# Nine selections per group moved from GpSimd to VectorE, the counting of the blocks put first, and three fp32r warm-up products

## The chip, the cores and the metric

One core of a Trainium2 chip. The metric is the device time of one execution in microseconds (us); lower is better. The engines are named as in the profile: PE is TensorE (PEld its weight loads), DVE is VectorE, ACT is ScalarE, POOL is GpSimd, SP is SyncE, which here only starts transfers.

## The reference

A linear attention with exponential features over 8 batches, 8 heads and 576 positions feeds a mixture of 8 experts that takes, for each of its 4608 tokens, the one expert with the largest logit.

```python
def phi(x):
    proj = np.einsum('bhsd,df->bhsf', x, w_phi)
    proj = proj - np.max(np.abs(proj), axis=-1, keepdims=True)
    return np.concatenate([np.exp(proj), np.exp(-proj)], axis=-1)
q_p, k_p = (phi(q), phi(k))
kv = np.einsum('bhsf,bhsd->bhfd', k_p, v)
z = np.sum(k_p, axis=2)
num = np.einsum('bhsf,bhfd->bhsd', q_p, kv)
den = np.einsum('bhsf,bhf->bhs', q_p, z)[..., None] + 1e-06
...
logits = x @ w_gate                       # x: num / den, 4608 x 512
expert_idx = np.argmax(logits, axis=1)
...
    h = np.maximum(xe @ w1[e], 0.0)       # xe: the tokens of expert e
    ye = h @ w2[e]
    out[mask] = gate_w[mask, None] * ye
```

## The kernel before

**Attention.** The heads are worked in 16 units `u` of two heads for two batches, four units to a group, so that a group holds the nine 128-token tiles of two batches with all heads. Every float32 matrix is split into a rounded part and a remainder (names that end in `h` and `l`, or `_hi` and `_lo`), and a product is three products: high by high, high by low, low by high. In a unit `project` (L253 to L260) multiplies a tile of k or q by the weights into the PSUM tile `ps_proj` (two buffers); DVE takes the largest magnitude `mx` (L259) and subtracts it (`t`, L260); ACT takes the exponentials. For k, ACT rounds them to `kh` (L280) and DVE or POOL subtracts to `kl` (L282); for q, PE transposes `t` into `pt` (L291) first. PE sums k by v in `pk` (L334), the sums are multiplied with a constant in `pf` (L360), DVE copies them to `kf` (L370), and `pn` (L382) multiplies the q features with `kf`. `normalize` (L409 to L418) divides on DVE. POOL splits the inputs (`xl`, L242).

**Routing.** When a group's four units are done, `route` turns its logits into a choice of expert and a rank of each token within its expert. For the first three groups (`final` is None) its steps are spread between the products of the next group's first unit, so one falls near 145, 245 and 345 us. The last of these steps are nine calls of `select(c)` (L734), one per tile: each makes two bfloat16 matrices of 128x128 from the row `iota_pb` and the tile's ranks `rkr`, `sel_p` on DVE and `sel_h` on POOL. The last group is routed by two more calls, `r1` and `r2`, in the transition to the experts (about 415 to 450 us); there some selections are made on ACT, and the four others stay as they are.

**Transition.** From the counts of all tokens, `place` (L552 to L589) works out which blocks of 128 rows belong to which expert; `block_of` (L909 to L928) gives each token its block as the matrix `bsel`; `tokens_of` (L935 to L944) sums 72 small products of `sel_p` and `sel_h` with `bsel` into `pp`, from which DVE reads the token lists `gidx` and `sidx`; `experts_of` (L946 to L964) finds the expert of each block: four compares into `eg` (L955, DVE), two steps on POOL (L961, L962), and the sum `eidx` (L964, DVE). The SP queue reads `eidx` before it starts the conditional weight transfers of the pair of blocks 2 (L981, L984).

**Experts.** Blocks are worked in pairs. `gather` fetches the rows of a block by `gidx` with a transfer that POOL issues (L845); `x_parts` transposes them (`px`, L1021) and splits them to `xh` (L1023, ACT) and `xl` (L1024, DVE); `pair_first` multiplies by the first matrix (`pm`, L1041 to L1043) and splits the result to `hh`, `hl` (L1049); `pair_second` multiplies by the second (`po`, L1061 to L1063); `write` scales and scatters. `weights(u, k)` splits piece k (0 to 7) of an expert's matrices: `wh` on ACT (L998), `wl` (L999) on POOL for the pieces in a list, else on DVE. The first two pairs use an expert that was chosen early, whose weights and rows are there before the transition.

**Start.** Seven bfloat16 products of 512 columns (L118) into a scratch PSUM tile come ahead of the first projection.

**What sets the order.** The program is written in the order in which the steps are called; a scheduler then moves instructions within each engine by priorities and its own model of their lengths. `tc.high_priority` raises the priority of what is called in it; the kernel ties some orders by dependencies without a semaphore (`add_manual_dep`). Each engine then runs its list strictly in order.

Of the kernel before, what the change touches and what calls it, by code (L numbers as in the profile page):

```python
# [42 lines left out]
XW = DM + 4  # L43

WARM = 7
BIG = 8192.0


@with_exitstack
def tile_linear_attention_moe(  # L50
# [65 lines left out]
    for _ in range(WARM):  # L116
        pw = ps_kv.tile([P, 4, P], F32, name="pw", tag="pk")
        T.matmul(pw, ones, ones.unsqueeze(1).to_broadcast([P, 4, P]), start=True, stop=True)  # L118
    iota_i = const.tile([P, P], I32, name="iota_i")
    iota_p = const.tile([P, P], F32, name="iota_p")  # L120
    iota_pb = const.tile([P, P], BF16, name="iota_pb")
# [313 lines left out]

    behind_order = [None]

    def ordered(items):


        def go(f):
            m = f()
            if behind_order[0] is not None:
                tc.add_manual_dep(
                    m.ins,
                    behind_order[0].ins.name,
                    mybir.DependencyInfo(mybir.DependencyClass.NoSync, mybir.DependencyReason.DATA),
                    reason="order of the products",
                )
            behind_order[0] = m  # L450

        return [(t, lambda f=f: go(f)) for t, f in items]
# [141 lines left out]
    def route(g, lgc, c0, n, final=None):  # L594
# [77 lines left out]
        def count():  # L672
            if final:
                pc = ps_kv.tile([P, E], F32, name="pc", tag="pk")
                T.matmul(pc, ones, r["base_b"], start=True, stop=False)
                for c in range(n):
                    T.matmul(pc, ones, r["oh_b"][:, c, :], start=False, stop=(c == n - 1))
                place(pc)

        def sum_up():  # L680
            if not final:
# [48 lines left out]
        def select(c):  # L730
            if final is not None and c0 + c in ON_ACT:
                return select_a(c)
            for eng, dst, by in ((V, sel_p, part1), (G, sel_h, hbase[:, j0 + c : j0 + c + 1])):
                eng.tensor_scalar(  # L734
                    dst[:, j0 + c, :], iota_pb, r["rkr"][:, c : c + 1], by, op0=ALU.is_equal, op1=ALU.mult
                )
# [198 lines left out]
    def tokens_of():  # L935

        pp = ps_kv.tile([P, NB], F32, name="pp", tag="pk")
        for j in range(NTILE):
            T.matmul(pp, sel_p[:, j, :], bsel[:, j, :], start=(j == 0), stop=False)
            T.matmul(pp, sel_h[:, j, :], bsel[:, j, :], start=False, stop=(j == NTILE - 1))  # L940
        V.tensor_scalar(gidx, pp, -1.0, 0.0, op0=ALU.add, op1=ALU.max)
        emp = sg.tile([P, NB], F32, name="emp")
        V.tensor_scalar(emp, pp, 0.5, BIG, op0=ALU.is_lt, op1=ALU.mult)
        V.scalar_tensor_tensor(sidx, pp, -1.0, emp, op0=ALU.add, op1=ALU.add)  # L944

    def experts_of():  # L946
        ends = sg.tile([1, 2, E], F32, name="ends")
# [4 lines left out]
        places = ((first[0:1], ends[:, 0], 0, 2 * NPAIR), (start[0:1], ends[:, 1], 2 * NPAIR, NB))  # L952
        for low, high, n0, n1 in places:
            for j, edge in enumerate((low, high)):
                V.tensor_tensor(  # L955
                    eg[:, j, n0:n1],
                    iota_p[0:1, n0:n1].unsqueeze(2).to_broadcast([1, n1 - n0, E]),
                    edge.unsqueeze(1).to_broadcast([1, n1 - n0, E]),
                    op=ALU.is_ge,
                )  # L960
        G.tensor_tensor(eg[:, 0], eg[:, 0], eg[:, 1], op=ALU.subtract)  # L961
        G.tensor_tensor(eg[:, 0], eg[:, 0], iota_e[0:1].unsqueeze(1).to_broadcast([1, NB, E]), op=ALU.mult)  # L962
        with nc.allow_low_precision("experts are integers"):
# [3 lines left out]
    st = {}  # L967
    lim = [NU_ALWAYS]

    POOL_LO0, POOL_LO = (1, 3, 7), (3, 7)  # L970

    def blocks(u):
        return [2 * u, 2 * u + 1] if u < NPAIR else [u + NPAIR]
# [13 lines left out]
    def weights(u, k):  # L987
# [8 lines left out]
        th = pool.tile([P, FF], F32R, name="wh", tag=f"wh{slot}")  # L996
        tl = pool.tile([P, FF], F32R, name="wl", tag=f"wl{slot}")
        A.copy(th, raw[k])  # L998
        (G if k in (POOL_LO if u else POOL_LO0) else V).tensor_tensor(tl, raw[k], th, op=ALU.subtract)  # L999
        for j in range(2) if u == 0 else [u]:  # L1000
            st["w", j, k] = (th, tl)
        if u > 0:
# [46 lines left out]
        V.scalar_tensor_tensor(hl, pm, 0.0, hh, op0=ALU.max, op1=ALU.subtract)  # L1049
        st["hp", u, j] = (hh, hl)  # L1050

    def pair_second(u, j):
        if j == 0:
            pools = ((ps_o, "po") if u else (ps_t, "pht"), (ps_t, "pht"))
            st["po", u] = [p.tile([P, DM], F32, name="po", tag=t) for p, t in pools]
        hh, hl = st["hp", u, j]
        th, tl = st["w", u, KD + j]
        for i in range(2):
            for t, po in enumerate(st["po", u]):
                r, c = slice(t * P, (t + 1) * P), slice(i * DM, (i + 1) * DM)  # L1060
                T.matmul(po, hh[:, i, r], th[:, c], start=(i == j == 0), stop=False)  # L1061
                T.matmul(po, hh[:, i, r], tl[:, c], start=False, stop=False)  # L1062
                T.matmul(po, hl[:, i, r], th[:, c], start=False, stop=(i == 1 and j == 3))  # L1063
        if j == 3:
            for b, po in zip(blocks(u), st["po", u]):
                write(b, po)

# [102 lines left out]
    late.close()  # L1170
    ps_o = ctx.enter_context(tc.tile_pool(name="ps_o", bufs=2, space=PSUM, side="left", reuse_waits="tile"))
    wpr = ctx.enter_context(tc.tile_pool(name="wpr", bufs=1, side="left", reuse_waits="tile"))
    x_parts(1, 1)
    for k in range(NPC):
        load_weights(2, k)
    weights(2, 0)
# [3 lines left out]
    for u in range(1, NPAIR):  # L1180
        for j in range(4):
            pair_first(u, j)
            if j > 1:
                x_parts(u + 1, j - 2)
            pair_second(u - (j == 0), (j - 1) % 4)
            if j == 0:
                gather(u + 1)
            for du, k in AHEAD_W[j]:
                weights(u + du, k)
# [106 lines left out]
```

## Time and profile before

| | |
|---|---|
| median of 3 runs | 923.04 us (922.51 to 923.66) |
| the profiled execution | 922.39 us |
| its span (first to last instruction) | 920.5 us |
| mean granted clock of TensorE | 0.993 |
| busy: PE, PEld, DVE, ACT, POOL | 892.2, 834.6, 586.1, 592.4, 491.6 us |

The span is what the views of the trace divide; 1.9 us of the profiled execution lie around it. A busy time is the time in which the engine had an instruction under way; where the table says that an instruction waited, the name after the arrow is the instruction whose end released it. In the rows of a timeline, `x6` says that six instructions of a kind are drawn together, and the second number is then the time from the start of the first to the end of the last.

### The profile page before, as it was taken

The page shows a single profiled execution, that of the slowest core. Times are in us where ns is not written, and L with a number is a line of the kernel's source. Part 1 is how long each engine was busy: PE and PEld are TensorE (multiplying, and loading weights), DVE is VectorE, ACT ScalarE, POOL GpSimd, SP SyncE. Part 2 cuts the span into 40 slices and gives each one's busy share as a digit, 9 for nine tenths or more (in the row PEclk, how much of TensorE's full clock was granted, in tenths as well). Part 3 has the DMA queues.
Part 4 walks back from the last instruction along what each step waited for, and adds up shares of the span by engine and source line. Part 5 has one row for each costly group of instructions (what it writes and reads, how often), then busy time and mean ns, then how long its engine had stood idle before and what let it go on. Part 6 is the DMA issues. An engine that isn't in the chain of part 4 may idle for free. (4 is left out here: it accounts for less than half of the span.)

```text
span 920.5 us, 18442 instructions
## 1 busy us (share of the span) xinstructions
PE 892.2 (97%) x6831; PEld 834.6 (91%) x6831; DVE 586.1 (64%) x1037; ACT 592.4 (64%) x900; POOL 491.6 (53%) x335
## 2 busy tenths in 40 slices
PE   7999999999999999998999999999999999999995
PEld 6999999999999999997899999999999999987883
DVE  7777779777977788759744444444444444457850
ACT  6987776777777876654555555555555555568951
POOL 6766669666886668644543343333333333336641
PEclk9999999999999999999999999999999999999997
DMA  4243333333333343351152243431434634663100
GB/s 155 82 118 107 107 106 90 101 108 107 94 81 92 92 122 79 107 162 30 58 181 94 68 143 118 145 123 41 148 112 158 219 114 147 227 208 123 46 24 15
DMA packets 64621, 102.45 MB, mean 111 GB/s; under 512 B 10703, under 2 KB 28623, under 8 KB 64529
## 3 DMA queue, kind: packets, MB, share of 16 engines
q1 hardware_dynamic: 57136, 80.31, 28.3%
q0 software_dynamic: 6720, 20.80, 7.5%
q8 instruction: 54, 0.88, 0.4%
q14 instruction: 39, 0.31, 0.1%
q10 hardware_dynamic: 672, 0.15, 0.1%
HBM read 136.81 MB, written 20.26 MB: 171 GB/s over the span
## 5 line engine op out<-in xcount | busy, mean ns | idle before, releaser
L999 DVE TENSOR_TENSOR wl<-raw,wh 128x1024 fp32r<-128x1024 f32 x137 | 185.9, 1369 | 139.1 <-ACT wh L998 139.1
L998 ACT CAST wh<-raw 128x1024 fp32r<-128x1024 f32 x184 | 191.6, 1050 | 96.8 <-PE po L1063 68.3
L999 POOL TENSOR_TENSOR wl<-raw,wh 128x1024 fp32r<-128x1024 f32 x47 | 116.6, 2486 | 174.9 <-ACT wh L998 167.4
L382 PE MATMUL pn<-kf,qp 128*128 128x73 f32 x1024 | 155.2, 254 | 4.4 <-DVE kf L370 4.4
L1041 PE MATMUL pm<-xh,wh 128*128 128x256 f32 x544 | 153.7, 283 | 0.7 <-ACT xh L1023 0.7
L1042 PE MATMUL pm<-xl,wh 128*128 128x256 f32 x544 | 154.1, 283 | 0.2 <-DVE xl L1024 0.2
L1043 PE MATMUL pm<-xh,wl 128*128 128x256 f32 x544 | 154.0, 283 | 0.0
L382 PEld LDWEIGHTS pn<-kf,qp 128*128 128x128 f32 x1024 | 148.7, 190 | 5.4 <-DVE kf L370 5.2
L259 DVE TENSOR_REDUCE mx<-ps_proj 128x4 f32<-128x512 f32 (+1 forms) x160 | 100.7, 630 | 62.3 <-PE ps_proj L255 62.2
L282 POOL TENSOR_TENSOR kl<-e,kh 128x1024 fp32r<-128x1024 f32 x47 | 112.2, 2387 | 37.4 <-ACT kh L280 37.4
L242 POOL TENSOR_TENSOR xl<-xr,xh 128x512 fp32r<-128x512 f32 (+2 forms) x63 | 88.7, 1409 | 72.0 <-ACT xh L241 72.0
L1061 PE MATMUL po<-wh,hh 128*128 128x512 f32 x272 | 109.1, 401 | 0.0
L1062 PE MATMUL po<-wl,hh 128*128 128x512 f32 x272 | 106.8, 393 | 2.3 <-DVE wl L999 2.3
L1041 PEld LDWEIGHTS pm<-xh,wh 128*128 128x128 f32 x544 | 104.1, 191 | 3.7 <-ACT xh L1023 0.9
L1042 PEld LDWEIGHTS pm<-xl,wh 128*128 128x128 f32 x544 | 104.1, 191 | 2.8 <-DVE xl L1024 0.4
L1063 PE MATMUL po<-wh,hl 128*128 128x512 f32 x272 | 106.1, 390 | 0.0
L1043 PEld LDWEIGHTS pm<-xh,wl 128*128 128x128 f32 x544 | 104.2, 191 | 0.0
L260 DVE TENSOR_TENSOR t<-ps_proj,mx 128x512 f32<-128x512 f32 (+1 forms) x160 | 101.3, 634 | 3.5
L334 PE MATMUL pk<-kl,vh 128*65 128x256 f32 x320 | 97.0, 303 | 1.4 <-DVE kl L282 1.2
L334 PE MATMUL pk<-kh,vh 128*65 128x256 f32 x320 | 97.9, 306 | 0.4
L334 PE MATMUL pk<-kh,vl 128*64 128x256 f32 x320 | 97.5, 305 | 0.0
L1111 POOL DMA_INDIRECT out<-ob,sidx x41 | 46.4, 1131 | 91.4 <-ACT ob L1109 85.5
(229 smaller groups left out, 2054.0 us busy)
## 6 DMA issues: line engine op xcount, KB each, us to landing
raw<-w SPq DMA_DIRECT2D x184, 512.0 KB
vt<-vv SPq DMA_DIRECT2D x15, 640.0 KB
x_dram<-xrow SPq DMA_DIRECT2D x30, 256.0 KB
xr<-kT SPq DMA_DIRECT2D x15, 320.0 KB
xr<-qT SPq DMA_DIRECT2D x15, 320.0 KB
xr<-kT SPq DMA_DIRECT2D x17, 256.0 KB
xr<-qT SPq DMA_DIRECT2D x17, 256.0 KB
x_dram<-xrow SPq DMA_DIRECT2D x32, 32.0 KB
```

The costliest lines, as they stand in the source:

```text
L260: V.tensor_tensor(t[:, 0 : 2 * n, :], psv, mx[:, 0 : 2 * n].unsqueeze(2).to_broadcast([P, 2 * n, F]), op=ALU.subtract,)
L282: eng.tensor_tensor(kl, e[:, 0:m], kh, op=ALU.subtract)
L334: return T.matmul(st["pk", bb][0:n, hh, :], (vl if j == 1 else vh)[:, 2 * (c + (bb if c == 8 else 0)) + hh, 0:n], (kl if j == 2 else kh)[: ...
L382: m = T.matmul(st["pn"][:, 2 * (c % 3) + hh, :], qp[:, s, s0 + hh, :] if c < 8 else qp[:, s, hh, bb : bb + 2].rearrange("p b q -> p (b q)" ...
L998: A.copy(th, raw[k])
L999: (G if k in (POOL_LO if u else POOL_LO0) else V).tensor_tensor(tl, raw[k], th, op=ALU.subtract)
L1041: T.matmul(pm[:, i], th, xh[:, k, :], start=(k == 0), stop=False)
L1042: T.matmul(pm[:, i], th, xl[:, k, :], start=False, stop=False)
L1043: T.matmul(pm[:, i], tl, xh[:, k, :], start=False, stop=(k == KD - 1))
L1061: T.matmul(po, hh[:, i, r], th[:, c], start=(i == j == 0), stop=False)
L1062: T.matmul(po, hh[:, i, r], tl[:, c], start=False, stop=False)
L1063: T.matmul(po, hl[:, i, r], th[:, c], start=False, stop=(i == 1 and j == 3))
```

## The change

Six edits. (1) Three products of `w_hi` by itself, 128 columns each, follow the seven warm-up products. (2) `place` is called with its priority raised by 150. (3) The early groups' `sel_h` are made on DVE, as `sel_p` is: 27 instructions. (4) A helper `behind` ties one instruction behind another on its engine without a semaphore; with it the four `eg` compares and the `wl` of piece 7 of pair 0 come behind the write of `sidx`. (5) That `wl` of piece 7 moves from POOL to DVE. (6) `pair_second(0, 3)` is called in two halves, one ahead of `x_parts(1, 1)` and one behind it, and no longer in the loop of pair 1.

```diff
+NWARM = 3
...
         T.matmul(pw, ones, ones.unsqueeze(1).to_broadcast([P, 4, P]), start=True, stop=True)
+    pw = ps_kv.tile([P, 4, P], F32, name="pw", tag="pk")
+    for i in range(NWARM):
+        T.matmul(pw[:, i], w_hi[:, 0:F], w_hi[:, F : 2 * F], start=(i == 0), stop=(i == NWARM - 1))
...
+    def behind(m, other):
+
+        tc.add_manual_dep(
+            m.ins,
+            other.ins.name,
+            mybir.DependencyInfo(mybir.DependencyClass.NoSync, mybir.DependencyReason.DATA),
+            reason="order of the engine",
+        )
...
-                place(pc)
+                with tc.high_priority(offset=150):
+                    place(pc)
...
-            for eng, dst, by in ((V, sel_p, part1), (G, sel_h, hbase[:, j0 + c : j0 + c + 1])):
+            E2 = V if final is None else G
+            for eng, dst, by in ((V, sel_p, part1), (E2, sel_h, hbase[:, j0 + c : j0 + c + 1])):
...
-        V.scalar_tensor_tensor(sidx, pp, -1.0, emp, op0=ALU.add, op1=ALU.add)
+        st["places"] = V.scalar_tensor_tensor(sidx, pp, -1.0, emp, op0=ALU.add, op1=ALU.add)
...
-                V.tensor_tensor(
+                m = V.tensor_tensor(
                     eg[:, j, n0:n1],
...
+                behind(m, st["places"])
...
-    POOL_LO0, POOL_LO = (1, 3, 7), (3, 7)
+    POOL_LO0, POOL_LO = (1, 3), (3, 7)
...
-        (G if k in (POOL_LO if u else POOL_LO0) else V).tensor_tensor(tl, raw[k], th, op=ALU.subtract)
+        m = (G if k in (POOL_LO if u else POOL_LO0) else V).tensor_tensor(tl, raw[k], th, op=ALU.subtract)
+        if (u, k) == (0, KD + 3):
+            behind(m, st["places"])
...
-    def pair_second(u, j):
+    def pair_second(u, j, half=None):
...
-        for i in range(2):
+        for i in range(2) if half is None else [half]:
...
-        if j == 3:
+        if j == 3 and half != 0:
...
+    pair_second(0, 3, 0)
     x_parts(1, 1)
+    pair_second(0, 3, 1)
...
-            pair_second(u - (j == 0), (j - 1) % 4)
+            if (u, j) != (1, 0):
+                pair_second(u - (j == 0), (j - 1) % 4)
```

What this does to the order is more than the diff shows, since the scheduler places anew. Line numbers of the changed kernel are 4 to 18 higher. Three places:

**DVE where the selections of the first group stand.** Before, from the division of the last unit on, two selections being already ahead:

```order
L410 RECIPROCAL rec<-rec 128x6
L734 TENSOR_SCALAR sel_p<-iota_pb,rkr,part_145 128x128
L412 TENSOR_TENSOR xrow<-pn,rec 128x384
L418 TENSOR_TENSOR lgc<-pn,rec 128x3x16
L734 TENSOR_SCALAR sel_p<-iota_pb,rkr,part_145 128x128 x6
L259 TENSOR_REDUCE mx<-ps_proj 128x2
L260 TENSOR_TENSOR t<-ps_proj,mx 128x256
L409 TENSOR_SCALAR rec<-pn 128x6
L410 RECIPROCAL rec<-rec 128x6
L259 TENSOR_REDUCE mx<-ps_proj 128x2
L412 TENSOR_TENSOR xrow<-pn,rec 128x384
L418 TENSOR_TENSOR lgc<-pn,rec 128x3x16
L260 TENSOR_TENSOR t<-ps_proj,mx 128x256
L282 TENSOR_TENSOR kl<-e,kh 128x512
L259 TENSOR_REDUCE mx<-ps_proj 128x4
L370 COPY kf<-pf 128x292
```

and in the changed kernel, four selections (two of each kind) being already ahead:

```order
L414 RECIPROCAL rec<-rec 128x6
L749 TENSOR_SCALAR sel_p<-iota_pb,rkr,part_149 128x128
L416 TENSOR_TENSOR xrow<-pn,rec 128x384
L422 TENSOR_TENSOR lgc<-pn,rec 128x3x16
L749 TENSOR_SCALAR sel_h<-iota_pb,rkr,hbase 128x128
L749 TENSOR_SCALAR sel_p<-iota_pb,rkr,part_149 128x128
L749 TENSOR_SCALAR sel_h<-iota_pb,rkr,hbase 128x128
L749 TENSOR_SCALAR sel_p<-iota_pb,rkr,part_149 128x128
L749 TENSOR_SCALAR sel_h<-iota_pb,rkr,hbase 128x128
L749 TENSOR_SCALAR sel_p<-iota_pb,rkr,part_149 128x128
L749 TENSOR_SCALAR sel_h<-iota_pb,rkr,hbase 128x128
L263 TENSOR_REDUCE mx<-ps_proj 128x2
```

```order
L264 TENSOR_TENSOR t<-ps_proj,mx 128x256
L374 COPY kf<-pf 128x292
L286 TENSOR_TENSOR kl<-e,kh 128x512
L761 TENSOR_REDUCE pse<-ex 128x9
L263 TENSOR_REDUCE mx<-ps_proj 128x4
```

The `mx` of 128x2 that stood behind 9 selections now stands behind 12; the last six are spread over the rows behind it, the first of them between this `mx` and its `t`. The copy `kf` (now L374), which stood behind a `kl` of 128x512 and an `mx`, now stands ahead of that `kl`.

**POOL at the same place.** Before:

```order
L242 TENSOR_TENSOR xl<-xr,xh 128x640
L282 TENSOR_TENSOR kl<-e,kh 128x1024
L242 TENSOR_TENSOR xl<-xr,xh 128x512
L734 TENSOR_SCALAR sel_h<-iota_pb,rkr,hbase 128x128 x6
L282 TENSOR_TENSOR kl<-e,kh 128x1024
L734 TENSOR_SCALAR sel_h<-iota_pb,rkr,hbase 128x128 x3
L242 TENSOR_TENSOR xl<-xr,xh 128x512
```

and in the changed kernel:

```order
L246 TENSOR_TENSOR xl<-xr,xh 128x640
L286 TENSOR_TENSOR kl<-e,kh 128x1024
L246 TENSOR_TENSOR xl<-xr,xh 128x512
L286 TENSOR_TENSOR kl<-e,kh 128x1024
L246 TENSOR_TENSOR xl<-xr,xh 128x512
```

The second `kl` stood behind six selections and now stands directly behind `xl`.

**DVE in the transition.** Before, from the reduction that follows the second `wl` to the token lists:

```order
L914 TENSOR_REDUCE at<-si_t 128x36
L1049 SCALAR_TENSOR_TENSOR hl<-pm,hh 128x512
L918 TENSOR_SCALAR turn<-at 128x36
L919 TENSOR_SCALAR late_at<-at 128x36
L964 TENSOR_REDUCE eidx<-eg 1x43
L920 TENSOR_SCALAR at<-at 128x36
L922 TENSOR_TENSOR bi<-blk,turn 128x36
L923 TENSOR_TENSOR late_at<-late_at,at 128x36
L925 TENSOR_TENSOR blk<-blk,at 128x36
L924 TENSOR_TENSOR bi<-bi,late_at 128x36
L926 TENSOR_TENSOR bi<-bi,blk 128x36
L928 TENSOR_TENSOR bsel<-iota_p,bi 128x516 x3
```

and in the changed kernel, from `bsel` on:

```order
L943 TENSOR_TENSOR bsel<-iota_p,bi 128x516 x3
L956 TENSOR_SCALAR gidx<-pp 128x43
L958 TENSOR_SCALAR emp<-pp 128x43
L959 SCALAR_TENSOR_TENSOR sidx<-pp,emp 128x43
L1015 TENSOR_TENSOR wl<-raw_6063,wh 128x1024
L970 TENSOR_TENSOR eg<-iota_p,first 1x272
L970 TENSOR_TENSOR eg<-iota_p,ends 1x272
L970 TENSOR_TENSOR eg<-iota_p,start 1x72
L970 TENSOR_TENSOR eg<-iota_p,ends 1x72
L1042 TENSOR_TENSOR xl<-px,xh 128x4x128
L980 TENSOR_REDUCE eidx<-eg 1x43
```

The four compares into `eg`, which stood among the rows of `place` (up to 14 rows ahead of the first piece shown), and `eidx`, which stood ahead of `bsel`, now come behind `sidx`; so does the `wl` of piece 7, which was POOL's, right behind `sidx` and ahead of the compares. On POOL the gather of block 2 (L845), which stood behind L961, L962 and that `wl`, now stands ahead of L961 and L962 (now L977, L978). On PE the 72 products `pp` come four products of `po` and one transposition earlier; behind them stand four `po`, the four transpositions `px` of one block, six `po`, the four `px` of the block that was gathered, six `po`, and only then the first `pm`; before it was three `px`, twelve `po`, four `px` and then directly `pm`.

## Rows read from the trace of the kernel before

**Rows 1.** From the first page of the profile: busy time of each engine over the span, with its share and its number of instructions.

```profile
PE 892.2 (97%) x6831; PEld 834.6 (91%) x6831; DVE 586.1 (64%) x1037; ACT 592.4 (64%) x900; POOL 491.6 (53%) x335
```

**Rows 2.** Stretches of the span: start and end, length, then busy time of each engine (with its instructions), granted clock of PE (1.00 is the higher of its two levels), share of the DMA engines and GB/s.

```profile
0.00:20.00 20.00, 15.42 (x71) 11.64 (x72) 13.73 (x32) 13.01 (x23) 12.35 (x38) 0.91 0.52 165
...
140.00:160.00 20.00, 18.34 (x170) 17.94 (x169) 18.50 (x44) 12.63 (x24) 18.72 (x17) 1.00 0.32 96
160.00:180.00 20.00, 20.00 (x190) 19.99 (x188) 14.08 (x32) 14.84 (x26) 13.38 (x7) 1.00 0.47 124
...
340.00:360.00 20.00, 18.37 (x171) 17.94 (x169) 18.78 (x46) 12.55 (x24) 18.73 (x17) 1.00 0.32 97
420.00:440.00 20.00, 17.39 (x116) 14.65 (x116) 19.59 (x88) 10.27 (x23) 9.09 (x9) 1.00 0.10 19
```

**Rows 3.** What PE waited for: the line that waited, the instruction that released it, us in total, times, the longest.

```profile
PE pn L382 <- DVE kf L370: 4.4, 3, 1.5
PE po L1062 <- DVE wl L999: 2.3, 1, 2.3
...
PE pm L1041 <- ACT xh L1023: 0.7, 1, 0.7
```

**Rows 4.** Timeline of DVE in the first of the three stretches with selections: start, length, engine, line, operation, output and input, and in brackets the idle time before it and what ended it.

```profile
144.34 2.50 DVE L734 TENSOR_SCALAR sel_p<-iota_pb,rkr,part 128x128 bf16<-128x128 bf16 x2
...
147.19 0.54 DVE L412 TENSOR_TENSOR xrow<-pn,rec 128x384 f32<-128x384 f32 x1
...
147.76 1.56 DVE L734 TENSOR_SCALAR sel_p<-iota_pb,rkr,part 128x128 bf16<-128x128 bf16 x6
149.25 0.41 DVE L259 TENSOR_REDUCE mx<-ps_proj 128x2 f32<-128x256 f32 x1
149.76 0.42 DVE L260 TENSOR_TENSOR t<-ps_proj,mx 128x256 f32<-128x256 f32 x1
...
151.69 2.75 DVE L282 TENSOR_TENSOR kl<-e,kh 128x512 fp32r<-128x512 f32 x1
...
154.96 0.45 DVE L370 COPY kf<-pf 128x292 f32<-128x292 f32 x1
```

**Rows 5.** Timeline of POOL in the same stretch.

```profile
143.17 2.38 POOL L282 TENSOR_TENSOR kl<-e,kh 128x1024 fp32r<-128x1024 f32 x1
145.51 1.27 POOL L242 TENSOR_TENSOR xl<-xr,xh 128x512 fp32r<-128x512 f32 x1
146.78 4.75 POOL L734 TENSOR_SCALAR sel_h<-iota_pb,rkr,hbase 128x128 bf16<-128x128 bf16 x6
151.51 2.38 POOL L282 TENSOR_TENSOR kl<-e,kh 128x1024 fp32r<-128x1024 f32 x1
```

**Rows 6.** Timeline of PE in the same stretch.

```profile
150.33 0.37 PE L253 MATMUL ps_proj<-w_hi,xh 128*128 128x256 f32 x1
...
152.43 0.34 PE L360 MATMUL pf<-fold,kvT 65*128 65x73 f32 x2
...
155.46 0.44 PE L382 MATMUL pn<-kf,qp 128*128 128x73 f32 x2 [1.50 <-DVE kf L370]
```

**Rows 7.** Timeline of DVE in the transition.

```profile
432.84 4.27 DVE L999 TENSOR_TENSOR wl<-raw,wh 128x1024 fp32r<-128x1024 f32 x1
...
438.17 0.49 DVE L964 TENSOR_REDUCE eidx<-eg 1x43 int32<-1x344 f32 x1
...
439.48 1.91 DVE L928 TENSOR_TENSOR bsel<-iota_p,bi 128x516 bf16<-128x516 f32 x3
442.25 0.20 DVE L941 TENSOR_SCALAR gidx<-pp 128x43 int32<-128x43 f32 x1 [0.86 <-PE pp L940]
```

**Rows 8.** Timeline of POOL in the transition.

```profile
432.68 1.03 POOL L962 TENSOR_TENSOR eg<-eg,iota_p 1x344 f32<-1x344 f32 x1
433.67 2.36 POOL L999 TENSOR_TENSOR wl<-raw,wh 128x1024 fp32r<-128x1024 f32 x1
442.73 1.14 POOL L845 DMA_INDIRECT xg<-x_dram,gidx  x1 [6.70 <-DVE emp L943]
```

**Rows 9.** Timeline of PE in the transition.

```profile
437.17 0.50 PE L1062 MATMUL po<-wl,hh 128*128 128x512 f32 x1 [2.29 <-DVE wl L999]
437.51 0.40 PE L1063 MATMUL po<-wh,hl 128*128 128x512 f32 x1
437.74 0.39 PE L1061 MATMUL po<-wh,hh 128*128 128x512 f32 x1
...
446.23 0.66 PE L1021 MATMUL px<-ident,xg 128*128 128x128 f32 x4 [0.91 <-DMA xg<-x_dram,gidx]
```

**Rows 10.** One stretch of DVE from the first weights of pair 2 to the last split that pair 2 needs (columns as in Rows 2).

```profile
444.10:468.50 24.40, 22.59 (x149) 20.17 (x148) 17.82 (x17) 16.70 (x22) 11.87 (x7) 1.00 0.33 99
```

**Rows 11.** Timeline of DVE at the end of that stretch: the split itself.

```profile
467.78 0.68 DVE L1024 TENSOR_TENSOR xl<-px,xh 128x512 fp32r<-128x512 f32 x1
```

**Rows 12.** Timeline of PE at the start: the second and third product of the first projection, and two later projections that waited.

```profile
4.34 0.41 PE L254 MATMUL ps_proj<-w_lo,xh 128*128 128x256 f32 x1
4.55 0.41 PE L255 MATMUL ps_proj<-w_hi,xl 128*128 128x256 f32 x1
...
6.60 0.58 PE L253 MATMUL ps_proj<-w_hi,xh 128*128 128x256 f32 x1 [1.02 <-DVE t L260]
...
13.14 0.41 PE L253 MATMUL ps_proj<-w_hi,xh 128*128 128x256 f32 x1 [1.21 <-DVE t L260]
```

## The prediction

> **What bounds the kernel now.** The busy times come first: PE is busy 892.2 of 920.5 us [rows 1], so PE is the bound, and a change is worth what it does to the 28 us in which PE has nothing under way. The stretches tell where these lie: the first 20 us (4.6 us idle), the three stretches with the selections of an early group (1.66 us in the first of them, 1.63 in the last), and the transition (2.6 us in one of its slices) [rows 2]. Between them PE is full; in the 20 us behind a selection stretch it is busy 20.00 of 20.00 us [rows 2], so a loss in an earlier stretch isn't made up later, and nor is a gain lost. The waits then name the causes: `kf` three times, 4.4 us in all; one `wl` of 2.3 us; `xh` 0.7 [rows 3]; the gathered rows 0.9 [rows 9]. The change works at all of these places, and each has its own cost, so I follow the timelines there. A measurement of this kernel can tell about 0.2% (1.85 us) from no change.
>
> **The selections (edit 3), 27 instructions.** Why does `kf` come late? DVE starts a `kl` of 128x512 at 151.69 which takes 2.75 us, and only then `mx` and, at 154.96, the copy [rows 4]; PE has waited 1.50 us when `pn` starts at 155.46 [rows 6]. That `kl` ends 0.6 us after POOL's `kl`, which ran from 151.51 [rows 5]. The first selections show the same: two `sel_p` take 2.50 us, the first ending as POOL's `kl` ends and the second as POOL's `xl` ends, while six of them take 1.56 us (0.26 each) beside POOL's `sel_h` [rows 4, 5]. So here a subtraction on POOL holds up a DVE instruction that has its operands in SBUF, a `sel_h` does not, and DVE gets in for one instruction where two POOL subtractions meet.
>
> The Trainium skill ("SBUF — State Buffer", section "SBUF: two separate sides") calls the port pair that VectorE and GpSimd share an exclusive lock: who starts first keeps it for the whole instruction. For the subtractions the rows agree; for the `sel_h`, beside which six `sel_p` passed undelayed [rows 4, 5], they do not. If the `sel_h` held DVE up as well, each of those six would have taken the 0.79 us of a `sel_h`, and taking the `sel_h` off POOL would be worth some 3 us of DVE time per group; by the rows it frees nothing on DVE.
>
> Now the new order. DVE's first two selections wait as before, to 145.6 and 146.8. POOL no longer has six `sel_h` (4.75 us [rows 5]) ahead of its second `kl`, so that one starts at 146.78 rather than 151.51 and holds DVE's third selection until about 149.2. Then come nine selections (0.26 each, 2.3 us), and `xrow` and its neighbours (0.6 to 0.7), ahead of the `mx` that was at 149.25: it comes at about 152.2. One more selection stands between it and its `t`, which ends at about 153.2, where it ended at 150.18 [rows 4]. PE wanted that tile's buffer at 150.33 for its next projection [rows 6]: a new wait of 2.9 us. The rest of PE's work up to `pn` shifts with it: the last `pf`, at 152.43 [rows 6], goes to 155.3; `kf`, which now stands ahead of the DVE `kl`, is written by about 156, and `pn`, due at 153.96 + 2.9 = 156.9, no longer waits. Against 155.46 that is +1.4 us; part of it (0.3 by estimate) is covered because PE's new order takes `pf` and `pk` products ahead of the next transpositions. I take **+1.1 a group, +3.3 for three**; the third stretch has the same idle time as the first, and `kf` was late three times [rows 2, 3]. Ends: the 1.65 us vanish with nothing in their place (-5.0 for three), or DVE is held up once more by a POOL subtraction, 2.75 - 0.68 = 2.07 us each (the `kl` against an `mx`-sized instruction of the same 512 elements, as `xl` at 467.78 took [rows 4, 11]), +9.5 for three. I take the middle because it follows the row-by-row order. POOL loses 22 us of work that nothing waited for.
>
> **Transition (edits 2, 4, 5, 6).** PE waits 2.29 us at 437.17 [rows 9] for a `wl` that DVE held from 432.84 for 4.27 us [rows 7], while POOL ran L962 to 433.7 and the `wl` of piece 7 from 433.67 for 2.36 us [rows 8]. Edits 4 and 5 take both POOL instructions out of that time (L962 stands behind the compares); the `wl` then takes about 1.2 us and PE's wait goes: -2.3. The chain to `bsel` (439.48 [rows 7]) moves up by 3.05 us there and 0.4 for `eidx` taken from ahead of it (438.17 [rows 7]), to about 436.0. PE reaches `pp` at 440.2 less 0.3 (its wait for `bsel`), 2.29 and about 1.0 (four `po`, whose starts lie 0.23 apart [rows 9], and a transposition stand behind now), 436.6, when the first third of `bsel` is just there: -0.3. The gather is POOL's next work as before, and its rows reached PE at 446.23, 4.0 us after `gidx` began at 442.25 [rows 7, 9], so some 4.2 us after `pp`. Behind `pp` PE has four `po`, four `px` and six `po`, 2.6 us, so it waits about 1.6 us there rather than 0.91 [rows 9]; the six `po` behind that `px` (1.4 us) hide the waits for `xh` and `xl` (0.7 [rows 3] and 0.2): -0.2 for the two together. The moved `wl` of piece 7 is written about 1.8 us after `pp`, and PE gets to it after 1.7: +0.1. The pieces give -2.7; place's higher priority brings `spot` a little earlier, and I take **-2.8**, ends -3.8 (all of the PE waits here gone) and -1.0 (the wait for `bsel` takes the place of the one for `wl`). Of the four `eg` compares 1.3 us leave the chain ahead of `bsel`; `place` raised costs nothing, being the same instructions.
>
> **Pair 2 (what edits 4 and 5 put off).** `eidx` comes behind `sidx`, a `wl`, four compares and, on POOL, the gather (1.14) and L961 and L962 (2 to 3 us): some 7 to 8 us later by these lengths than at 438.17 [rows 7, 8]. SP and ACT start pair 2's pieces after that, so DVE's work from 444.18 is put off by as much. In that stretch DVE is busy 17.82 of 24.40 us [rows 10], so 6.6 us are slack, and the split that PE needs next ends at 468.46 [rows 11], 0.4 us before PE uses it. 7 to 8 less 7.0 leaves 0 to 1.0 us: **+0.4**; ends 0 and +4 (two of the `wl` meeting a POOL one).
>
> **Start (edit 1).** Three products of 128 columns come ahead of the first projection, whose products of 256 columns start 0.21 us apart [rows 12]; three of 128 then cost 0.3 to 0.6 us. PE waits at 6.60 and 13.14 for `t` on DVE [rows 12], which is fed by these projections, so the delay passes on; the reordering behind it can win some of it back. The granted clock over the first 20 us is 0.91 [rows 2]: some 1.8 us are lost to the lower level (1.2 against 2.4 GHz). Whether three short products change that no row shows; ends -1.5 and +1.2. I take **+0.2**.
>
> **Sum.** 0.2 + 3.3 - 2.8 + 0.4 = +1.1 us. Against the profiled execution's 922.39 us that is 923.5; this execution lies 0.65 us below the median, and on the median of 923.04 the forecast is **924.1 us**, within what can't be told from no change.
>
> **Rivals.**
> A, slower: DVE loses the openings. It gets in between two POOL subtractions only if it wins the port at that instant. It did at 145.5 and 146.8 [rows 4, 5], but the 4.27 us `wl` began beside L962 and was still waiting when POOL's `wl` ended [rows 7, 8], so it lost once. POOL now has `kl`, `xl`, `kl` back to back. With one more hold of 2.07 us in each stretch: 924.1 + 6.2 = 930.3 us. It decides if the second selection ends after 149.
>
> B, faster: the selections slip through. If POOL's second `kl` lets several of DVE's short selections pass before it takes the port, `mx` comes only some 0.8 us later (three selections of 0.26), the projection waits 0.75 us, and the 1.5 us for `kf` are gone: -0.8 a group instead of +1.1, 924.1 - 5.7 = 918.4 us; with no new wait at all 915.8. For it: nothing in the trace shows a queue of short DVE instructions at such an opening [rows 4]. Against it: two openings let in exactly one each.
>
> C, slower: pair 2 waits. `eidx` is late and two `wl` of pair 2 run beside POOL's: +3.6 more, 927.7 us. Against it: 6.6 us of slack [rows 10].
>
> **Chances.** Forecast 0.42 (its own range 921.5 to 926.5), A 0.13, B 0.30, C 0.15. The range from 916.5 to 931 us takes in A and B's middle, and leaves out B's end, and A together with C. Faster by over 0.2% is nearly all of B and a little of the forecast: 0.33. Same: most of the forecast and a little of B and C, 0.30. Slower: A, most of C and the upper part of the forecast, 0.37.
>
> **What would show it.** Right: PE's waits for `kf` and for the `wl` in the transition are gone; in their place stand three waits of a projection for `t` of 2 to 3 us and one for the gathered rows of 1 to 2 us; three selections of each early group take over 1 us, the third over 2; the three stretches show PE busy about 17.2 of 20 us rather than 18.35. Wrong: PE busy over 19 us in these stretches (B); a `wl` wait still in the transition; a wait of several us at the first product of pair 2 (C); the first 20 us off by more than 1.5 us.

## The result and the profile after

The changed kernel took **928.60 us** (median of 5 runs, 927.37 to 929.49) against 923.33 us (922.51 to 924.98) for the kernel before on the same chip: ratio 1.0053, 95% interval 1.0040 to 1.0067. The forecast was 924.1 us in a range of 916.5 to 931; the kernel became slower by 0.5%, which was one of the outcomes foreseen (with a chance of 0.37), and the likeliest number was 4.5 us too low. The profiled execution took 927.37 us with a span of 925.7 us, 5.2 us longer than the one before.

Busy times over the span, from the page of the changed kernel:

```profile
PE 895.4 (97%) x6834; PEld 837.8 (91%) x6834; DVE 590.8 (64%) x1065; ACT 592.3 (64%) x900; POOL 466.5 (50%) x307
```

Against [rows 1] POOL lost 25 us and PE *gained* 3.2 us, although the change adds only three short products to PE. Idle time of PE grew from 28.3 to 30.3 us. So of the 5.2 us only 2.0 are waits; the rest lies in PE's busy time, in which nearly the same work takes longer. Where, the stretches tell (columns as in [rows 2]):

```profile
0.00:20.00 20.00, 14.65 (x88) 11.20 (x88) 14.22 (x33) 14.83 (x27) 14.07 (x38) 1.00 0.50 142
...
140.00:160.00 20.00, 17.75 (x169) 17.61 (x168) 18.80 (x51) 11.36 (x22) 9.84 (x6) 1.00 0.32 96
160.00:180.00 20.00, 19.45 (x181) 18.93 (x181) 14.40 (x33) 15.86 (x28) 15.17 (x9) 1.00 0.39 108
240.00:260.00 20.00, 17.76 (x154) 17.61 (x153) 17.53 (x47) 10.53 (x20) 10.12 (x5) 0.91 0.32 97
260.00:280.00 20.00, 19.44 (x183) 18.93 (x182) 14.50 (x31) 16.18 (x26) 14.61 (x9) 1.00 0.26 66
340.00:360.00 20.00, 17.67 (x161) 17.33 (x161) 17.97 (x46) 12.46 (x21) 12.09 (x8) 0.93 0.33 94
360.00:380.00 20.00, 19.51 (x163) 18.98 (x163) 16.28 (x42) 15.47 (x26) 10.27 (x7) 0.90 0.19 45
420.00:440.00 20.00, 19.69 (x166) 18.74 (x165) 19.51 (x82) 11.19 (x25) 8.40 (x8) 1.00 0.29 87
440.00:460.00 20.00, 18.99 (x173) 16.16 (x172) 14.73 (x32) 9.46 (x14) 8.68 (x8) 1.00 0.20 60
460.00:480.00 20.00, 19.30 (x124) 17.31 (x123) 16.57 (x14) 12.55 (x16) 7.69 (x3) 1.00 0.29 93
```

The three stretches of the selections: idle 2.25 + 0.55 = 2.80 us in the first (20 less PE's busy time in each of its two rows), 2.80 in the second, 2.82 in the third, where it was 1.66, 1.65 and 1.63 in the kernel before. But look at the granted clock as well: 0.91 in the row of 240 us, 0.93 and 0.90 in the two of 340 and 360. It was 1.00 in each of these before. The transition goes the other way: 0.31 and 1.01 us idle, where it was 2.61 and 1.95. Behind it 0.70 us are new. Two rows of the kernel before that [rows 2] leaves out:

```profile
240.00:260.00 20.00, 18.35 (x171) 17.95 (x170) 18.36 (x43) 12.67 (x25) 18.75 (x17) 1.00 0.32 97
...
440.00:460.00 20.00, 18.05 (x181) 16.20 (x180) 15.46 (x18) 13.32 (x17) 11.29 (x7) 1.00 0.22 67
```

What PE waited for in the changed kernel:

```profile
PE ps_proj L257 <- DVE t L264: 8.0, 5, 2.2
...
PE pf L364 <- ACT kvT L355: 1.5, 3, 0.5
...
PE px L1039 <- DMA xg<-x_dram,gidx: 1.0, 1, 1.0
PE pm L1060 <- DVE xl L1042: 0.7, 1, 0.7
...
PE pn L386 <- DVE kf L374: 0.2, 1, 0.2
```

The waits for `kf` and for `wl` of [rows 3] are gone (0.2 us of the first is left); three of the five waits for `t` are the new ones, 2.2 us each, and in each stretch `pf` then waits another 0.5 us for a copy on ACT. DVE in the first stretch shows how they come about, line for line against [rows 4]:

```profile
144.72 1.26 DVE L749 TENSOR_SCALAR sel_p<-iota_pb,rkr,part 128x128 bf16<-128x128 bf16 x1
145.90 1.32 DVE L749 TENSOR_SCALAR sel_h<-iota_pb,rkr,hbase 128x128 bf16<-128x128 bf16 x1
147.14 2.41 DVE L749 TENSOR_SCALAR sel_p<-iota_pb,rkr,part 128x128 bf16<-128x128 bf16 x1
149.48 0.30 DVE L749 TENSOR_SCALAR sel_h<-iota_pb,rkr,hbase 128x128 bf16<-128x128 bf16 x1
...
152.13 0.41 DVE L263 TENSOR_REDUCE mx<-ps_proj 128x2 f32<-128x256 f32 x1
...
152.69 0.41 DVE L264 TENSOR_TENSOR t<-ps_proj,mx 128x256 f32<-128x256 f32 x1
...
155.06 0.46 DVE L374 COPY kf<-pf 128x292 f32<-128x292 f32 x1
```

and POOL against [rows 5]:

```profile
143.56 2.37 POOL L286 TENSOR_TENSOR kl<-e,kh 128x1024 fp32r<-128x1024 f32 x1
145.89 1.27 POOL L246 TENSOR_TENSOR xl<-xr,xh 128x512 fp32r<-128x512 f32 x1
147.13 2.37 POOL L286 TENSOR_TENSOR kl<-e,kh 128x1024 fp32r<-128x1024 f32 x1
```

The first selection ends as POOL's `kl` ends, the second as `xl` ends, and the third lasts 2.41 us, to the end of the second `kl`, which POOL now starts at 147.13. The fourth, with POOL idle, takes 0.30. `mx` comes at 152.13, `t` ends at 153.1 and `kf` is copied at 155.06.

The lower clock shows in PE's rows around the second of these waits:

```profile
254.54 0.43 PE L257 MATMUL ps_proj<-w_hi,xh 128*128 128x256 f32 x1 [2.24 <-DVE t L264]
254.77 0.41 PE L258 MATMUL ps_proj<-w_lo,xh 128*128 128x256 f32 x1
254.98 0.41 PE L259 MATMUL ps_proj<-w_hi,xl 128*128 128x256 f32 x1
...
258.48 0.28 PE L258 MATMUL ps_proj<-w_lo,xh 128*128 128x256 f32 x1
258.60 0.28 PE L259 MATMUL ps_proj<-w_hi,xl 128*128 128x256 f32 x1
```

Behind the wait of 2.24 us the products of 256 columns start 0.21 us apart, from 258.5 on 0.12. The granted clock of the trace is at its lower level (1.2 GHz) from 254.7 for 3.4 us here and from 357.1 for 6.8 us in the third stretch; in the first stretch of this execution it stayed up, with a wait as long. In the profile of before it is at its lower level only near the start and in the last 10 us.

The start of the same PE instruction, in each kernel against the kernel before, adds it up (the n-th product of its line, in us, plus for later; the head gives its start in the kernel before; the kernels below the first row are those of the experiments):

| | start, 129.2 | 1st stretch, 198.4 | 2nd, 298.5 | 3rd, 415.9 | transition, 464.2 | pair 2, 480.0 | last product, 908.2 |
|---|---|---|---|---|---|---|---|
| the change | +0.38 | +1.59 | +4.39 | +8.61 | +4.65 | +5.58 | +5.19 |
| the change, second profile | +1.31 | +4.09 | +8.24 | +11.10 | +7.20 | +8.32 | +7.86 |
| selections back on POOL | +1.15 | +1.16 | +1.18 | +1.21 | -2.70 | -1.61 | -2.05 |
| selections alone | +0.46 | +1.66 | +6.02 | +8.83 | +9.95 | +9.94 | +9.52 |
| POOL padded | +1.60 | +4.66 | +6.14 | +9.14 | +5.17 | +6.26 | +5.83 |
| PE's wait part filled | +1.79 | +3.28 | +4.99 | +7.16 | +3.31 | +4.40 | +4.15 |
| warm-up alone | +0.38 | +0.36 | +0.38 | +0.43 | +1.80 | +1.78 | +1.43 |
| transition alone | +0.18 | +0.18 | +0.18 | +0.18 | -3.39 | -2.30 | -2.29 |
| `kl` to POOL, selections back | +1.79 | +0.41 | -0.90 | -2.08 | -5.96 | -4.87 | -5.15 |
| `eg` untied, selections back | +1.54 | +1.52 | +1.53 | +1.55 | -0.37 | -0.37 | -0.80 |
| transition and `kl` to POOL | -0.46 | -0.40 | -1.64 | -2.79 | -6.60 | -5.50 | -5.33 |

The first row: start +0.38, stretches +1.21, +2.80 and +4.22, transition -3.96, pair 2 +0.93, tail -0.39. The idle time of a stretch grew by 1.14 to 1.19 us, and the first stretch costs that much; the other two cost 1.65 and 3.03 us more, and these are the stretches with the lower clock.

### The profile page after: what moved, and what is told of

It is laid out like the page before. It is cut to its first block, busy times and chain, and to the rows that moved or that the text cites. A ratio compares the mean times of both kernels' runs of the same rounds, so it can differ in the third digit from the quotient of the medians.

```text
span 925.7 us, 18444 instructions
## 1 busy us (share of the span) xinstructions
PE 895.4 (97%) x6834; PEld 837.8 (91%) x6834; DVE 590.8 (64%) x1065; ACT 592.3 (64%) x900; POOL 466.5 (50%) x307
## 5 line engine op out<-in xcount | busy, mean ns | idle before, releaser
L1015 POOL TENSOR_TENSOR wl<-raw,wh 128x1024 fp32r<-128x1024 f32 x46 | 114.4, 2492 | 173.1 <-ACT wh L1014 165.7
L257 PE MATMUL ps_proj<-w_hi,xh 128*128 128x256 f32 x288 | 91.1, 317 | 8.0 <-DVE t L264 8.0
```

What stands on the lines that cost most here:

```text
L1015: m = (G if k in (POOL_LO if u else POOL_LO0) else V).tensor_tensor(tl, raw[k], th, op=ALU.subtract)
```

## The experiments

Each was timed in five rounds beside the kernel before, except the last. Theory: the selections on VectorE cost 1.2 us of waiting per group because a POOL subtraction holds up the third of them; those waits let the clock fall, which costs some 4.6 us more in all; the transition gains about 4 and gives 1 back.

**Selections back on POOL (edit 3 undone).**

```diff
-            E2 = V if final is None else G
+            E2 = G
```

> The changed kernel with the early groups' sel_h back on GpSimd; all other edits stay. Theory (the selections on VectorE make PE wait 1.2 us more in each of three stretches, and these waits bring the granted clock down for 4.6 us of PE's work; the rest of the change gains 3.0 us): 920.3 us, kf late by 1.5 us three times as before, no fall of the clock near 255 and 357 us. Rival (the falls of the clock come from the other edits or from chance): 924 to 925 us, with the falls still there.

Measured: 920.14 us (919.03 to 920.5), ratio 0.9972 (0.9960 to 0.9984). The three waits for `kf` are back at 1.5 us; the clock does not fall between 27 and 910 us. Edit 3 alone thus turns a kernel that is 0.3% faster than before into one that is 0.5% slower.

**Selections alone (edit 3 on the kernel before).** The reverse:

```diff
-            for eng, dst, by in ((V, sel_p, part1), (G, sel_h, ...
+            for eng, dst, by in ((V, sel_p, part1), (V if final is None else G, sel_h, ...
```

> The kernel before with nothing but the early groups' sel_h on VectorE. Theory: 923.3 + 3.6 for three waits of a projection for t + up to 4.6 for the clock, so 927 to 931.5 us, with falls of the clock at the second or third stretch. Rival (the selections cost only the waits): 926.9 us and no fall.

Measured: 932.19 us (931.04 to 932.91), ratio 1.0103 (1.0088 to 1.0118): 9.6 us, a little over the theory's upper end. The clock was low for 6.8 us in the second stretch and 3.4 in the third, and for 3.4 from 445.7, behind the wait for `wl` of 2.3 us, which this kernel still has (+1.1 in the table). That a wait in the transition can do the same I had not expected.

**POOL padded.** POOL makes the nine selections once more, into a part of `sel_h` that the last group overwrites. The rows of all other engines are the same, one by one:

```diff
+            if final is None:
+                G.tensor_scalar(sel_h[:, (NG - 1) * NC + c, :], iota_pb, r["rkr"][:, c : c + 1], ...)
             for eng, dst, by in ((V, sel_p, part1), (E2, sel_h, ...
```

> The changed kernel, and GpSimd makes the nine selections of an early group a second time, into a part of sel_h that is overwritten later; the order of all other engines is the same row by row. GpSimd's second kl then stands behind six of them as in the kernel before. Theory (that kl holds VectorE's third selection up for 2.1 us, which is what makes PE wait): the third selection takes 0.3 us, PE's three waits of 2.2 us for t fall to under 0.8, no fall of the clock: 917 to 921 us. Rival (VectorE simply has nine instructions more ahead of t): the waits stay over 1.8 us and the time at 928 us.

Measured: 926.71 us (925.04 to 928.03), ratio 1.0040 (1.0027 to 1.0054). The time was missed, and the traces say why. DVE in the first stretch:

```profile
148.37 0.51 DVE L758 TENSOR_SCALAR sel_p<-iota_pb,rkr,part 128x128 bf16<-128x128 bf16 x1
...
151.73 0.41 DVE L263 TENSOR_REDUCE mx<-ps_proj 128x2 f32<-128x256 f32 x1
...
153.28 0.17 DVE L414 RECIPROCAL rec<-rec 128x6 f32<-128x6 f32 x1
153.37 2.30 DVE L758 TENSOR_SCALAR sel_p<-iota_pb,rkr,part 128x128 bf16<-128x128 bf16 x1
```

POOL there:

```profile
148.38 4.88 POOL L749 TENSOR_SCALAR sel_h<-iota_pb,rkr,hbase 128x128 bf16<-128x128 bf16 x6
153.22 2.37 POOL L286 TENSOR_TENSOR kl<-e,kh 128x1024 fp32r<-128x1024 f32 x1
```

PE's waits from 140 to 180 us:

```profile
PE pt L295 <- DVE t L264: 1.7, 1, 1.7
PE ps_proj L257 <- DVE t L264: 0.6, 1, 0.6
```

With the `kl` behind six selections the third selection took 0.51 us and the projection waited 0.6 us rather than 2.2: that half holds. But the `kl` at 153.22 then caught another selection, at 153.37, for 2.30 us, and PE waited 1.7 us for the next `t`. The wait was moved and not removed, since a selection of DVE stands wherever that subtraction falls. Both theories' times are wrong here; that it is POOL's subtraction, and not the number of selections, that costs the 2 us, is shown by the order being the same on all engines but POOL. The clock fell here too, in the first and the third stretch, by the waits of 1.7 and 1.6 us.

**PE's wait part filled.** Four (`NFILL`) bfloat16 products with a zero matrix go into the running sum `pk` ahead of the projection that waits:

```diff
+        if x == "k" and c0 == 0 and st["u"] in (6, 10, 14):
+            for _ in range(NFILL):
+                T.matmul(last_pk[0][0 : D + 1]..., zero_b, ones.unsqueeze(1).to_broadcast([P, 4, P]),
+                         start=False, stop=False)
```

> The changed kernel with four bfloat16 products of 512 columns, which add zeros to a running sum, directly ahead of the projection that waits for t in each early group; they fill 0.9 of the 2.2 us. Theory (the idle time of PE makes the clock fall): the same waits less 0.9, no or fewer falls of the clock in the stretches: 924 to 926 us. Rival (the falls have nothing to do with that idle time): 928.6 us with the same falls.

Measured: 926.43 us (925.88 to 929.42), ratio 1.0050 (1.0037 to 1.0063). PE in the first stretch:

```profile
152.22 1.03 PE L258 MATMUL pk<-ones,zero_b 128*65 128x512 bf16 x4
154.58 0.38 PE L270 MATMUL ps_proj<-w_hi,xh 128*128 128x256 f32 x1 [1.34 <-DVE t L277]
```

The products take 1.03 us out of the wait, 1.34 are left, and in this profile the clock is at its higher level from 21 to 918 us: the three stretches cost 1.5, 1.7 and 2.2 us, 5.4 in all against 8.2 and 9.8 in the two profiles of the change. By the profile the theory holds. The median doesn't tell: the ratio is that of the change itself, within the intervals. The start was 1.4 us later than in the first profile of the change, and the scheduler placed `kf` behind `kl` and `mx` again, which explains part. In the other five executions no trace tells where the clock fell. Their mean granted clock is 0.988 to 0.991, where this one has 0.997, the five executions of the change 0.984 to 0.990 and the six of "selections back on POOL" 0.989 to 0.996: the ranges overlap, and a mean does not say at which stretch the clock was low. So that filling the wait saves the clock is shown for one execution only.

**Warm-up alone (edit 1 on the kernel before).**

```diff
+    pw = ps_kv.tile([P, 4, P], F32, name="pw", tag="pk")
+    for i in range(NWARM):
+        T.matmul(pw[:, i], w_hi[:, 0:F], w_hi[:, F : 2 * F], start=(i == 0), stop=(i == NWARM - 1))
```

> The kernel before with nothing but the three fp32r products at the end of the warm-up. Theory (they come ahead of the first projection and delay what VectorE needs from it): +0.4 to +1.2 us on 922.6, so 923.0 to 923.8, all of it in the first 50 us. Rival (they bring the clock up earlier and this pays): under 922 us.

Measured: 923.18 us (922.69 to 925.79), ratio 1.0005 (0.9995 to 1.0015): no difference that can be measured. In its profile the clock fell at 438.2 for 3.4 us, behind the wait for `wl` of 2.3 us, which gives the +1.80 of the table. In the eight profiles of kernels with these products the start is 0.4 to 1.8 us later (first column of the table), in the three others -0.5 to +0.5. The clock's first rise in the trace comes at 4.0 to 6.4 us in five of the eight and at about 20 in the other three ("POOL padded", "PE's wait part filled", "`kl` to POOL"), and at 4.7 to 10.1 in the four without the products; it varies between executions, and no run separates the products from that.

**Transition alone (edits 2, 4, 5 and 6 on the kernel before).**

> The kernel before with the edits of the transition alone (counting first, the eg compares and the wl of piece 7 behind sidx, that wl on VectorE, pair_second in halves); no new warm-up products, selections as before. Theory (the wl wait of 2.3 us and the order of PE there give 3.9, pair 2 takes 0.9 back): 919.2 to 919.8 us. Rival (part of the gain came with the other edits): 921 us or more.

Measured: 920.33 us (918.75 to 920.81), ratio 0.9960 (0.9947 to 0.9973). By the table -3.6 in the transition and +1.1 in pair 2. The time is 0.5 us over the theory and under the rival's bound.

**`eg` untied (selections back on POOL, the four compares free to stand ahead of `bsel`).**

```diff
-                behind(m, st["places"])
```

> The changed kernel with sel_h back on GpSimd and the four eg compares not tied behind sidx, so that eidx is ready as early as before. Theory (eidx came late and made pair 2 wait 0.9 us): the wait of the first product of pair 2 for xl goes, 919.2 us. Rival (that wait comes from the wl on VectorE and the order, not from eidx; or the compares ahead of bsel cost as much): 920 us or more.

Measured: 921.40 us (920.32 to 925.8), ratio 0.9985 (0.9974 to 0.9996). The first half of the theory holds: nothing is lost in pair 2 (-0.37 and -0.37 in the table). The second, the time of 919.2 us, is wrong, and the rival's last case came true: the compares ahead of `bsel` cost what the free `eidx` gains, and more. PE's waits from 420 to 480 us:

```profile
PE po L1079 <- DVE wl L1014: 1.0, 1, 1.0
```

A `wl` is late again by 1.0 us, and the transition gains 1.9 rather than 3.9. So the tie costs 1.1 us in pair 2 (from "selections back on POOL") and saves 2.0.

**`kl` to POOL (selections back on POOL; in the units 6, 10 and 14 the `kl` of 128x512 goes to POOL).**

```diff
-        eng = G if c0 in (4, 6) or (c0 == 0 and st["u"] > 0) else V
+        eng = G if c0 in (4, 6) or (c0 == 0 and st["u"] > 0) or (c0 == 8 and st["u"] in (6, 10, 14)) else V
```

> The changed kernel with sel_h back on GpSimd, and in the three units with selections the kl of 128x512 moved from VectorE to GpSimd, so that nothing on VectorE ahead of kf meets a subtraction of GpSimd. Theory (kf is late only because that kl is held up): PE's three waits of 1.5 us for kf go, 920.1 - 4.5 = 915.6 us. Rival (the projection behind it waits for its buffer instead, or xl on GpSimd comes late): 918 to 920 us.

Measured: 917.95 us (917.07 to 920.34), ratio 0.9948 (0.9936 to 0.9961). The three waits for `kf` are gone and the stretches gain 1.4, 1.3 and 1.2 us. This confirms the first step of the forecast, that this `kl` made `kf` late; that POOL held it up, and not its own length, the rows tell (2.75 us beside POOL's `kl` [rows 4, 5]), since this run takes it away from DVE altogether. The profiled execution took 917.07 us; its start was 1.8 us late.

**Transition and `kl` to POOL together, on the kernel before.**

> The kernel before with the edits of the transition and with the kl of 128x512 of the three units with selections on GpSimd; sel_h on GpSimd as before, no new warm-up products. Theory (the gains of the transition, 3.0 us, and of the three waits for kf, 1.5 us each, add; the warm-up products give nothing): 923.3 - 3.0 - 4.5 = 915.8 us, no wait for kf, no fall of the clock between 50 and 900 us. Rival (the warm-up products hold the gain at the start or the gains overlap): 918 us, as with them.

Measured: **917.22 us** (915.25 to 918.53), ratio 0.9933 (0.9920 to 0.9947), the lowest ratio of all, though its interval overlaps with that of "`kl` to POOL": faster than before by 0.7% and than the change by about 1.2% (0.9933 / 1.0053). It lies between theory and rival. The stretches in its profile:

```profile
140.00:160.00 20.00, 19.81 (x187) 19.67 (x184) 17.16 (x44) 14.75 (x28) 20.00 (x17) 1.00 0.31 97
160.00:180.00 20.00, 18.65 (x174) 18.22 (x173) 15.24 (x31) 12.64 (x23) 12.45 (x8) 1.00 0.47 123
240.00:260.00 20.00, 19.83 (x187) 19.68 (x186) 17.02 (x44) 14.78 (x28) 20.00 (x17) 1.00 0.32 97
340.00:360.00 20.00, 19.64 (x182) 19.25 (x181) 17.64 (x46) 14.62 (x27) 20.00 (x18) 1.00 0.32 97
```

PE's idle time falls to 0.2 to 0.4 us in the three, but the row of 160 us shows 1.35 us idle. There DVE has

```profile
160.12 3.26 DVE L282 TENSOR_TENSOR kl<-e,kh 128x1024 fp32r<-128x1024 f32 x1
```

a `kl` that takes 1.2 us alone and 3.26 here, beside POOL's subtractions, and PE then has a wait that the other two stretches lack:

```profile
PE ps_proj L253 <- DVE rec L409: 1.2, 1, 1.2
```

In the first group the gain is lost again (-0.46 to -0.40 in the table).

**The change again, unaltered, for a second profile.**

> The changed kernel once more, unaltered, for a second profile. Theory (the waits of 2.2 us in the three stretches make the clock fall, not in each execution at the same one): falls of 3.4 us or more at one to three of the stretches, and none elsewhere between 50 and 900 us; 927.4 to 929.5 us. Rival (the falls of the first profile were chance): none at the stretches.

Measured: one run, 930.06 us, 0.6 above the theory's upper end. The stretches:

```profile
140.00:160.00 20.00, 17.76 (x154) 17.62 (x153) 17.38 (x47) 10.05 (x20) 10.14 (x5) 0.91 0.31 96
...
240.00:260.00 20.00, 17.62 (x159) 17.29 (x158) 17.54 (x45) 12.14 (x22) 11.67 (x8) 0.91 0.32 95
260.00:280.00 20.00, 19.44 (x166) 18.92 (x165) 16.06 (x34) 15.77 (x27) 10.78 (x7) 0.92 0.21 50
340.00:360.00 20.00, 18.99 (x184) 18.61 (x182) 18.55 (x46) 14.55 (x25) 15.94 (x10) 1.00 0.32 99
360.00:380.00 20.00, 18.22 (x150) 17.70 (x151) 17.45 (x46) 14.37 (x25) 7.83 (x6) 0.91 0.22 53
```

The same waits of 2.2 us, and this time the clock fell in all three stretches (from 154.1 for 3.4 us, from 256.5 for 6.8, from 362.3 for 3.4); they cost 2.8, 4.2 and 2.9 us. Between 50 and 900 us it fell nowhere else.

Over the twelve profiles (ten of experiments and the two of before and after), between 50 and 900 us: waits of 2.2 or 2.3 us of PE (three each in the two profiles of the change and in "selections alone", and the `wl` of the transition in that one, in "warm-up alone" and in the kernel before) were followed by a fall 9 times in 12. Of the 21 waits of 1.3 to 1.7 us in the other profiles 2 were, both in "POOL padded", where another 0.6 us of waiting stands close by. A fall costs about half its length: 1.65 us for the 3.4 and 3.03 for the 6.8 of the first profile. The Trainium skill ("TensorE: Matmul & The Clock Gate", section "HAM oscillation — how this bites in real kernels") says that waits of PE inside a kernel bring its clock down and that the work behind them then runs at half speed. These rows agree in that, with products of 256 columns 0.21 rather than 0.12 us apart; but the waits in the skill's example are longer than any here, and these of 2.2 or 2.3 us were enough in 9 of 12 cases.

## Why the prediction was right or wrong

**Start, +0.2; measured +0.38.** Within its ends, though the second profile of the same kernel has +1.31, just past the end of +1.2; alone, the edit does nothing that can be measured. The 1.8 us that the forecast read from the granted clock of 0.91 are too few: ahead of the first rise (at 9.9 us in the profile of before) the trace holds no record of the clock, and a stretch counts that time as 1.00, while the products of 256 columns at 4.3 us stood 0.21 us apart [rows 12], as in the fall above. So the 1.00 of the changed kernel's first row is no gain either; its first rise comes at 5.6 us.

**Selections, +3.3 by waits; the waits came to +3.5.** Each step of the row-by-row working stands in the trace: the third selection held up to the end of the second `kl` (forecast 149.2, measured 149.5, with the start 0.4 later), a projection waiting for `t` by 2.2 us (forecast 2.9 less 0.3), no wait for `kf`. (The wait of `pf` for ACT, 0.5 us a stretch, was not forecast.) "POOL padded" shows that the POOL subtraction does it. The step that failed is what the forecast made of such a wait: it counted a wait at its length ("a loss in an earlier stretch isn't made up later, and nor is a gain lost") and looked at the granted clock in the start alone. Two of the three waits also let the clock fall, +1.65 and +3.03, together **+4.7 us**. Without it the terms measured are 0.38 + 3.5 - 3.96 + 0.93 - 0.39 = +0.5 us, against the forecast's +1.1: the clock makes up all of the 4.1 us by which the profiled execution's +5.2 lies above the forecast, and the other terms were together 0.6 too high. The median lies outside the forecast's own 921.5 to 926.5 us; that the whole range still holds it is in part luck, since its upper part was set by rival A and no term stood for the clock behind a wait.

**Transition, -2.8; measured -3.96.** The `wl` takes 1.22 us and PE no longer waits for it, `bsel` is there in time, `xh` and `xl` are hidden. DVE there:

```profile
441.08 1.22 DVE L1015 TENSOR_TENSOR wl<-raw,wh 128x1024 fp32r<-128x1024 f32 x1
...
443.88 1.91 DVE L943 TENSOR_TENSOR bsel<-iota_p,bi 128x516 bf16<-128x516 f32 x3
...
447.24 1.27 DVE L1015 TENSOR_TENSOR wl<-raw,wh 128x1024 fp32r<-128x1024 f32 x1
...
451.51 0.50 DVE L980 TENSOR_REDUCE eidx<-eg 1x43 int32<-1x344 f32 x1 [1.42 <-POOL eg L978]
```

and PE:

```profile
450.76 0.66 PE L1039 MATMUL px<-ident,xg 128*128 128x128 f32 x4 [1.01 <-DMA xg<-x_dram,gidx]
```

The wait for the gathered rows was forecast at 1.6 and is 1.01; the wait for the `wl` of piece 7 (0.1) doesn't show. The waits fall by 3.1 us (2.3 + 0.9 + 0.7 + 0.2 to 1.0), and the 0.3 us that the forecast gave to the wait of `pp` for `bsel` are gone; the remaining 0.6 of the 3.96 no wait explains, and it is left open.

**Pair 2, +0.4; measured +0.9.** `eidx` starts at 451.51 rather than at 438.17 [rows 7]: 13.3 us later, 8.7 of them beside PE's own shift of 4.6; forecast 7 to 8. The wait comes where it was placed, for `xl`, 0.70 us. "`eg` untied" shows that the tie causes it.

**The rivals.** A (DVE loses the openings, 930.3) lies close to the time, but not by its mechanism: the second selection ends at 147.2, and both openings were won. B did not happen: no short selections passed ahead of the second `kl`. C happened in a quarter of its size. No rival spoke of the clock after a wait.

## What to carry to other kernels

Where PE is busy without a break, a wait on it costs its length and may cost the clock as well: here waits of 2.2 or 2.3 us did in 9 of 12 cases, waits of 1.3 to 1.5 us in none of 18. Read the granted clock of each stretch beside its busy time, in more than one execution, before a wait is given a price. Splitting a wait is no sure cure: in "POOL padded", with 0.6 and 1.6 to 1.7 us in each stretch, the clock still fell in two of three. On VectorE's and GpSimd's side look for the instruction of VectorE that stands where GpSimd subtracts: taking work off GpSimd brought its next subtraction forward onto VectorE's line, and the cheaper cure for a late copy was to move the one held-up subtraction to GpSimd. Test the parts of a change alone: here one edit lost 7 to 10 us and hid the 2 to 3 that the others gained.

## What the runs showed of the hardware that was not expected

PE's clock fell to 1.2 GHz for 3.4 or 6.8 us behind 7 of the 9 such waits at the selections, and not the same ones in each execution of the same kernel: the first stretch kept its clock in one profile of the change and lost it in the other. GpSimd's subtractions held up a 128x128 bfloat16 selection of VectorE for up to 2.41 us, while beside GpSimd's own selections, of the same shape, one took at most 0.51 us ("POOL padded"), against 0.30 with GpSimd idle.
